# Transformer block on one core: epsilon inside the normalization statistics, waits sorted, and new instruction orders for four engines

## Chip, cores, metric

One core of one Trainium2 chip. The metric is the device time of one execution in microseconds (us). The kernel before takes 204.28 us, the median of 3 runs (204.25 to 204.39).

## The reference

The block takes x (1 x 2048 x 448, bf16) through linear attention with a feature map and then a gated MLP, each behind a normalization without weights:

```python
def _layernorm(x, axis=-1, eps=1e-5):
    return (x - mean(x)) / sqrt(var(x) + eps)

# attention, H = 16 heads of Dh = 28
q, k, v = split(x @ wqkv)
pq, pk = q @ w_phi, k @ w_phi                 # per head, 28 x 28
phi_q = concat(softmax(pq), softmax(-pq))
phi_k = concat(softmax(pk), softmax(-pk))
kv, z = phi_k^T v, sum_s phi_k
o = (phi_q kv) / (phi_q z + 1e-6)
A = o @ wo
# MLP, F = 1792
B = (sigmoid(x @ w_gate) * (x @ w_up)) @ w_down

h  = x + A(_layernorm(x))
h2 = h + B(_layernorm(h))
```

## The kernel before

The 2048 rows are 16 tiles of 128 rows; four tiles make a chunk of 512. Every step is an operation with a name, `op(engine, name, function, reads, writes)`. `Graph` derives the dependences from what is read and written. **The order on each engine is written out by hand** in `ORDER`, one string of names for each of SP (DMA issues), ACT, PE, DVE and POOL; each engine executes its string strictly in order. `Graph.emit` puts semaphore waits ahead of each operation: the list `o.waits` is walked in order, and each entry becomes one `wait_ge` on the engine's queue. In the kernel before, that list is sorted by the place of the producer in the program text, latest first. `schedule()` works out an order of all operations by passing over the engines again and again, without any times; `emit` uses it as `self.order`. Some operations allow several engines; the one whose string holds the name gets it.

The names that matter here, with t the tile:

- `x…` loads x. `bst t`, `agg t` (DVE, L514, L515) are `bn_stats` and `bn_aggr` of a tile; `ve1_a` adds EPS to the variance, `pow1_a` (POOL, L527) takes it to the power -0.5, `nm1_a` negates the mean, `nb1_a` multiplies the two for ACT. They run once for a group of tiles: 0, 1, 2, 3, 4 to 5, 6 to 7, 8 to 11, 12 to 15; a is the first tile. `xn t` (L540 on ACT, L543 elsewhere) writes the normalized tile to one of three slots of `xn_pad`; `xT t` transposes it, by PE and an evacuation `xT t e` for tiles 0 to 3, by a DMA on SP's queue after that (L553).
- `wT0..3` and their evacuations `wTe0..3` transpose the key weights; `w2m0_0..3` multiply them by `w_phi`, `w2e0_0..3` evacuate (L500). `w2m1`, `w2e1` do the same for the query weights. `warm0..9` are matmuls on zeros, with no use but to keep PE running.
- `ppa/ppb` and `vva/vvb` project keys and values for tiles 0 to 3 in pairs; `pva t`, `pvb t` do both for one tile from 4 on. The a and b halves write the same PSUM banks with other row halves of PE, so that b waits for a. `ek t` (ACT) takes both exponentials, `ss t`, `rs t` (DVE) their sums and reciprocals, `phi t` (POOL or DVE, L655) the product, `v1 t` copies v; `kva t`, `kvb t` (PE) add the tile to the key-value sums.
- `pqa/pqb c_i` project the queries of a chunk, `eq` (ACT) takes their exponentials. `kvzA..D` mask the sums into matmul operands; `qs` and `num t` are the queries' products with them; `rsm qq b c rden o` (DVE, `o` on POOL or DVE) normalize; `oT` transposes; `woa/wob` is the output projection, `h t` the residual. For tiles 0 and 1 the second normalization uses `bs2`, `ag2`, `ve`, `pow2`, `hn`, `hT`, as the first one; for the others `h` accumulates the sum, `nm` and `sq` follow.
- `ga c_f`, `gb c_f` are the gate and up projections of a group of tiles, `sig` and `hh` the gating, `dn/dp/dm` the down projection, `fin` and `out` the end.

Of the kernel before, what the change touches and what calls it, by code (L numbers as in the profile page):

```python
# [321 lines left out]
def build(nc, A_x, A_wqkv, A_w_phi, A_wo, B_w_gate, B_w_up, B_w_down, out):  # L322
# [10 lines left out]
    with ExitStack() as es:  # L333
# [183 lines left out]
        def rstd(ts):  # L517
# [3 lines left out]
            def fve(e):  # L521
                return e.tensor_scalar(ve1[:, a:b], mv1[:, a:b, 1], EPS, None, op0=ALU.add)  # L522
# [465 lines left out]
```

## Time and profile before

| what | us |
|---|---|
| median of 3 runs | 204.28 |
| profiled execution, first to last instruction | 202.8 |
| what lies around the span (204.28 less 202.8) | 1.5 |
| PE busy | 195.9 |
| DVE busy | 135.5 |
| ACT busy | 95.7 |
| POOL busy | 55.6 |
| first gate matmul `ga0_1` starts at | 60.59 |

The profile is of one execution whose own time is its span and the 1.5 around it; all times in the text count from the span's first instruction. Busy time is the union of an engine's instructions, so that PE counts as busy in the matmuls on zeros too. The granted PE clock is 1.000 throughout.

### The profile page before, as it was taken

The numbers are of one execution on the slowest core, as the hardware profiler recorded it, in microseconds if no ns is written. First come the engines' busy times: TensorE is split into PE (matmuls) and PEld (weight loads), VectorE is DVE, ScalarE is ACT, GpSimd is POOL, SyncE is SP. The second block draws the span as 40 slices with busy tenths as digits, with TensorE's granted clock in tenths as the row PEclk, the third lists the DMA queues.
The fourth block names the chain that finished last, engine by engine and source line by source line (L and its number), as shares of the span: only waits on it lengthen the run. The fifth ranks groups of instructions, "written<-read, shape, count | busy, mean of one in ns | idle before, by whom it ended". The sixth has DMA issues, their size and how long they took to land.

```text
span 202.8 us, 5881 instructions
## 1 busy us (share of the span) xinstructions
PE 195.9 (97%) x2508; PEld 109.4 (54%) x2508; DVE 135.5 (67%) x328; ACT 95.7 (47%) x191; POOL 55.6 (27%) x97
## 2 busy tenths in 40 slices
PE   7889999999979999999999999999999999999995
PEld 3734556665448776677444444444554555454443
DVE  5899999979998897858667967536432422272224
ACT  3887989988882527222333342324422212222220
POOL 5599699723144303700033020001400000000000
DMA  6985516849949411251004411030212000004003
GB/s 154 316 141 123 80 33 89 230 158 279 308 37 229 55 31 29 50 82 26 3 3 100 100 29 26 3 74 24 58 47 54 0 0 3 0 3 136 0 0 94
DMA packets 32867, 16.27 MB, mean 80 GB/s; under 512 B 25096, under 2 KB 31944, under 8 KB 32840
## 3 DMA queue, kind: packets, MB, share of 16 engines
q1 hardware_dynamic: 32336, 15.86, 34.9%
q8 instruction: 20, 0.33, 0.7%
q10 hardware_dynamic: 504, 0.03, 0.2%
q14 instruction: 7, 0.06, 0.1%
HBM read 8.34 MB, written 1.84 MB: 50 GB/s over the span
## 4 chain that ended last, share of the span: by engine, by line
PE 84%; DVE 8%; POOL 2%; DMA 2%; issue 1%; SPq 1%; ACT 0%; DVEq 0%
PE psum L305 78%; PE psum L909 5%; DVE st L514 2%; DMA x_sb<-in_A_x_dram 2%; DVE ss L645 2%; POOL o_pad L780 1%; DVE b_sb L771 1%; DVE xn_pad L543 1%; SPq L407 1%; DVE c_sb L774 1%; PE psum L507 0%; POOL xn_pad L543 0%; DVE rs L651 0%; DVE xnT L500 0%; POOL rst L527 0%
## 5 line engine op out<-in xcount | busy, mean ns | idle before, releaser
L305 PE MATMUL psum<-xnT,wg_sb 64*128 64x512 bf16 (+1 forms) x490 | 93.1, 334 | 0.3 <-DVE rden L776 0.2
L305 PE MATMUL psum<-xnT,wu_sb 64*128 64x512 bf16 (+1 forms) x490 | 92.9, 334 | 0.0
L881 ACT ACTIVATE sg_sb<-psum 128x512 bf16<-128x512 f32 (+1 forms) x70 | 34.8, 511 | 91.4 <-PE psum L305 90.9
L882 DVE SCALAR_TENSOR_TENSOR hhT<-sg_sb,psum 128x512 bf16<-128x512 bf16 (+1 forms) x70 | 38.9, 576 | 53.3 <-ACT sg_sb L881 53.0
L305 PEld LDWEIGHTS psum<-xnT,wg_sb 64*128 64x128 bf16 x490 | 44.4, 94 | 23.4 <-DVE hhT L882 4.8
L305 PEld LDWEIGHTS psum<-xnT,wu_sb 64*128 64x128 bf16 x490 | 44.4, 94 | 13.5
L305 PE MATMUL psum<-wd_sb,hhT 64*128 64x448 bf16 x336 | 36.8, 350 | 0.0
L305 PEld LDWEIGHTS psum<-wd_sb,hhT 64*128 64x128 bf16 x336 | 16.9, 94 | 15.1 <-DVE x_sb L806 0.5
L305 PE MATMUL psum<-Wk,xnT 64*128 64x448 bf16 x112 | 22.1, 351 | 0.3 <-ACT Wk L500 0.2
L305 PE MATMUL psum<-wv_sb,xnT 64*128 64x448 bf16 x112 | 22.2, 351 | 0.1
L815 POOL TENSOR_SCALAR ve<-ssq 128x1 f32<-128x1 f32 x11 | 2.6, 233 | 57.8 <-ACT junk L812 57.5
L655 POOL TENSOR_TENSOR phi<-hhT,rs 128x896 bf16<-128x896 bf16 x10 | 17.3, 1749 | 3.6 <-DVE ve L522 1.8
L645 DVE TENSOR_REDUCE ss<-hhT 128x32 f32<-128x896 bf16 x16 | 16.9, 1063 | 0.3 <-ACT hhT L642 0.3
L691 ACT ACTIVATE eq<-psum 120x1024 bf16<-120x1024 f32 x16 | 15.7, 1028 | 1.3 <-PE psum L305 1.1
L305 PE MATMUL psum<-xnT,Wq 64*120 64x512 bf16 x112 | 15.0, 385 | 0.1
L305 PE MATMUL psum<-wo_o,oT 64*128 64x448 bf16 x56 | 13.2, 350 | 0.0
L305 PE MATMUL psum<-wo_e,oT 64*128 64x448 bf16 x56 | 13.2, 349 | 0.0
L916 DVE SCALAR_TENSOR_TENSOR x_sb<-psum,x_sb 128x448 bf16<-128x448 f32 (+2 forms) x17 | 9.4, 591 | 2.7 <-PE psum L909 1.6
L909 PE MATMUL psum<-wd_sb,hhT 128*128 128x448 bf16 (+2 forms) x70 | 11.2, 316 | 0.0
L305 PEld LDWEIGHTS psum<-Wk,xnT 64*128 64x128 bf16 x112 | 7.8, 94 | 6.1 <-PE psum L305 0.5
L780 POOL TENSOR_TENSOR o_pad<-c_sb,rden 128x448 bf16<-128x448 bf16 x8 | 7.4, 935 | 11.1 <-DVE rden L776 11.0
L771 DVE TENSOR_TENSOR b_sb<-psum,qq 128x464 bf16<-128x464 f32 x16 | 10.2, 638 | 0.3
(99 smaller groups left out, 236.9 us busy)
## 6 DMA issues: line engine op xcount, KB each, us to landing
out_dram<-x_sb SPq DMA_DIRECT2D x15, 112.0 KB, 1.8
x_sb<-in_A_x_dram SPq DMA_DIRECT2D x7, 224.0 KB, 4.6
wd_sb<-in_B_w_down_dram SPq DMA_DIRECT2D x7, 224.0 KB, 4.4
wg_sb<-in_B_w_gate_dram SPq DMA_DIRECT2D x3, 448.0 KB, 5.5
wu_sb<-in_B_w_up_dram SPq DMA_DIRECT2D x3, 448.0 KB, 5.9
wv_sb<-in_A_wqkv_dram SPq DMA_DIRECT2D x2, 224.0 KB, 4.9
wk_sb<-in_A_wqkv_dram SPq DMA_DIRECT2D x2, 196.0 KB, 3.8
wo_e<-in_A_wo_dram SPq DMA_DIRECT2D x1, 336.0 KB, 3.2
```

The source lines that it names most:

```text
L305: p = e.matmul(o, lhsT=w, rhs=r, start=st, stop=sp, tile_position=(row, 0))
L514: op("dve", "bst%d" % t, lambda e: e.bn_stats(st1[:, t, :], x_sb[:, t, :]), r=[("x", t)], w=[("st1", t)])
L645: op("dve", "ss%d" % t, lambda e: e.tensor_reduce(ss[:, s, :].rearrange("p (b h) -> p b h", h=2), eks.rearrange("p b (d h) -> p b h d", h= ...
L655: return e.tensor_tensor(phi[:, sp, :, :, :].rearrange("p b a n -> p (b a) n")[:, :, 0:56].rearrange("p b (d h) -> p b d h", h=2), eks.rea ...
L691: op("act", "eq%d_%d%s" % (c, i, "pm"[sg]), lambda e, sg=sg: e.activation(eq[c][:, sg, 2 * i:2 * i + 2, :].rearrange("p g n -> p (g n)"), ...
L771: op("dve", "b%d" % t, lambda e: e.tensor_tensor(h3(b_sb), OMv[:, :, :, 0:EV], h2(qq)[:, :, :, None].to_broadcast([P, NB, 8, EV]), ALU.mul ...
L780: return e.tensor_tensor(o_pad[:, t % NO, off:off + D].rearrange("p (h d) -> p h d", h=H), c_sb[:, t % NS, :, 0:DH], rden[:, t % NS, :][:, ...
L815: op(("pool", "dve"), "ve%d" % t, lambda e: e.tensor_scalar(ve2[:, t:t + 1], ssq2[:, t:t + 1], 1.0 / D ** 3, EPS, op0=ALU.mult, op1=ALU.ad ...
L881: op("act", "sig" + nm, lambda e: e.activation(sg_sb[:, k, 0:N], bk(bg)[:, 0:N], ACT.Tanh, scale=0.5), r=[B(bg)], w=[("sg", k)])
L882: op("dve", "hh" + nm, lambda e: e.scalar_tensor_tensor(out=hhT[(t0 // 4) % NHH][:, ff, ns], in0=sg_sb[:, k, 0:N], scalar=1.0, in1=bk(bu)[ ...
L909: p = e.matmul(bk(b)[:, lo:hi], lhsT=hb[:, ff, TS(t)], rhs=wd_sb[:, ff, lo:hi], start=ff == 0, stop=ff == FT - 1)
L916: op("dve", "fin%d%s" % (t, nm), lambda e: e.scalar_tensor_tensor(out=h_sb[:, t, lo:hi], in0=bk(b)[:, lo:hi], scalar=0.5, in1=h_sb[:, t, l ...
```

## The change

`bn_stats` leaves six numbers for a tile, and `bn_aggr` combines them. The buffers get nine columns: the last three, written once by `steps`, are a third group with count 0, mean 0 and a sum of squares of D x EPS, so that the aggregated variance already contains EPS. `ve1` and, for tiles 0 and 1, `ve` are gone; `xn` subtracts the mean instead of adding a negated one, so `nm1` is gone; `nb1` is made per tile and only where `xn` runs on ACT, which is nowhere in the new orders. The waits of an operation are sorted: loads first, then by the place of the producer in `self.order`. ACT, PE, DVE and POOL get new orders up to the second gate group; behind what is shown here they are the same names in the same order. SP's order is the same.

```diff
     @staticmethod
+    def engine(name):
+        return next(e for e in ENGINES if name in ORDER[e].split())
...
         known = {e: {} for e in ENGINES}
+        rank = {i: n for n, i in enumerate(self.order)}
...
             o.waits = [j for j in o.waits if ops[j].dma is not None or ops[j].pos == last[ops[j].eng]]
+            o.waits.sort(key=lambda j: (ops[j].dma != "in", rank[j]))
...
-    "act": (
-        "wphi3 wphi2 wphi1 wphi0 par kvzones wTe0 wTe1 xT1e xT0e wTe2 w2e0_0 w2e0_1 w2e0_2 w2e0_3 xn3 xn4 ek0 ek1 "
-        "xn6 v1_1 v1_0 ek2 v1_2 v1_3 ek3 w2e1_1 w2e1_0 ek4 v1_4 w2e1_2 ek5 v1_5 ek6 v1_6 xn11 ek7 w2e1_3 xn12 ek8 "
-        "ek9 v1_9 ek10 v1_10 xn15 ek11 v1_11 ek12 v1_12 eq0_0m ek13 eq0_0p ek14 v1_14 ek15 v1_15 eq0_1p eq0_1m "
-        "eq1_0m kvzB eq1_0p eq1_1p eq1_1m eq2_0p oT0e oT1e eq2_1p eq2_0m eq2_1m h0 h1 eq3_0p eq3_0m eq3_1m eq3_1p "
-        "sig0_1 sig0_0 sig0_3 sig0_2 sig0_5 sig0_4 sq3 sq2 "
-        ...
+    "act": (
+        "wphi3 wphi2 wphi1 wphi0 kvzones wTe1 xT1e xT0e wTe3 w2e0_1 w2e0_3 xT3e ek0 ek1 v1_0 v1_1 ek3 ek2 v1_2 "
+        "v1_3 w2e1_1 w2e1_0 v1_4 ek4 ek5 v1_5 w2e1_2 w2e1_3 ek6 v1_6 ek7 v1_7 ek8 v1_8 ek9 v1_9 ek10 v1_10 ek11 "
+        "eq0_0p ek12 v1_12 ek13 v1_13 eq0_0m ek14 ek15 v1_15 eq0_1p eq0_1m eq1_0m kvzC kvzA eq1_0p eq1_1m eq1_1p "
+        "eq2_0p eq2_0m oT1e eq2_1p eq2_1m h1 h0 eq3_0m eq3_0p eq3_1p eq3_1m sig0_1 sig0_0 sig0_3 sig0_2 sig0_5 "
+        "sig0_4 sq2 sq3 "
+        ...
-    "pe": (
-        "warm0 warm1 warm2 wT0 wT1 xT1 warm3 xT0 warm4 warm5 wT2 w2m0_0 wT3 warm6 w2m0_1 w2m0_2 warm7 w2m0_3 "
-        "warm8 ppa0 warm9 ppb0 xT3 xT2 vva0 vvb0 ppa2 ppb2 vva2 vvb2 w2m1_0 w2m1_1 seed pva4 kva0 pvb4 pva5 "
-        "w2m1_2 w2m1_3 pvb5 pva6 kvb0 kva1 pvb6 kvb1 kva2 pva7 kvb2 kva3 pvb7 pva8 kvb3 kva4 pvb8 pva9 pqa0_0 "
-        "pvb9 pva10 kvb4 kva5 pvb10 kvb5 kva6 pva11 kvb6 kva7 pvb11 pva12 kvb7 kva8 pvb12 pqb0_0 pva13 kvb8 kva9 "
-        "pvb13 pva14 kvb9 kva10 pvb14 pva15 kvb10 kva11 pvb15 kvb11 kva12 pqa0_1 kvb12 pqb0_1 kva13 pqa1_0 kvb13 "
-        "kva14 pqb1_0 kvb14 kva15 kvb15 qs pqa1_1 num0 pqb1_1 num1 pqa2_0 num2 pqb2_0 pqa2_1 oT0 oT1 pqb2_1 num3 "
-        "woa0 wob0 num4 pqa3_0 pqb3_0 pqa3_1 num5 pqb3_1 hT0 hT1 num6 ga0_1 ga0_0 gb0_1 gb0_0 woa2 num7 ga0_3 "
-        "ga0_2 gb0_3 gb0_2 wob2 ga0_5 ga0_4 gb0_5 gb0_4 woa4 ga0_7 ga0_6 gb0_7 gb0_6 num8 wob4 "
-        ...
+    "pe": (
+        "warm0 warm1 wT1 wT0 warm2 xT1 warm3 warm4 warm5 warm6 warm7 xT0 wT2 wT3 w2m0_0 w2m0_1 w2m0_2 w2m0_3 "
+        "warm8 warm9 xT3 ppa0 ppb0 xT2 vva0 vvb0 ppa2 ppb2 vva2 w2m1_1 vvb2 seed w2m1_0 pva4 kva0 pvb4 pva5 kvb0 "
+        "kva1 pvb5 kvb1 pva6 w2m1_2 w2m1_3 pvb6 pva7 pqa0_0 pvb7 kva2 pva8 kvb2 kva3 pvb8 kvb3 pva9 kva4 pvb9 "
+        "kvb4 pva10 pqb0_0 pvb10 kva5 pva11 kvb5 kva6 pvb11 kvb6 pva12 kva7 pvb12 kvb7 pva13 kva8 pvb13 kvb8 kva9 "
+        "pva14 kvb9 kva10 pvb14 pva15 kvb10 kva11 pvb15 pqa0_1 kvb11 kva12 pqb0_1 pqa1_0 kvb12 kva13 pqb1_0 kvb13 "
+        "kva14 kvb14 kva15 kvb15 qs pqa1_1 num0 pqb1_1 num1 pqa2_0 num2 pqb2_0 pqa2_1 oT0 oT1 num3 pqb2_1 woa0 "
+        "wob0 num4 pqa3_0 pqb3_0 pqa3_1 num5 pqb3_1 hT1 hT0 num6 ga0_1 ga0_0 gb0_1 gb0_0 woa2 num7 ga0_3 ga0_2 "
+        "gb0_3 gb0_2 wob2 ga0_5 ga0_4 gb0_5 gb0_4 woa4 ga0_7 ga0_6 gb0_7 gb0_6 wob4 num8 "
+        ...
-    "dve": (
-        "zero bd0 mask2 bst1 agg1 ve1_1 bst0 agg0 nm1_0 xn1 xn0 bst2 agg2 bst3 agg3 bst4 bst5 wTe3 agg4 agg5 bst6 "
-        "bst7 agg6 agg7 bst10 ve1_6 agg10 nm1_6 bst8 bst11 bst9 agg8 xT3e agg11 agg9 xT2e nm1_8 ve1_8 ss0 ss1 rs0 "
-        "bst13 rs1 ss2 bst12 bst14 rs2 agg12 agg13 agg14 bst15 ss3 xn10 ss4 rs3 agg15 rs4 ve1_12 nm1_12 phi3 ss5 "
-        "rs5 v1_7 ss6 phi5 rs6 v1_8 ss7 ss8 rs7 rs8 phi7 ss9 rs9 ss10 rs10 ss11 rs11 ss12 rs12 v1_13 ss13 phi12 "
-        "rs13 ss14 rs14 ss15 phi14 rs15 phi15 kvzA kvzC kvzD rsm0 qq0 b0 c0 b1 rden0 c1 rsm2 rden1 qq2 b2 c2 "
-        "rden2 o2 rsm3 qq3 b3 c3 rden3 bs2_0 rsm4 ag2_0 qq4 bs2_1 b4 ag2_1 c4 hn0 rsm5 qq5 hn1 b5 hT1e c5 hT0e "
-        "rden4 rden5 rsm6 qq6 b6 c6 hh0_1 hh0_0 rsm7 rden6 qq7 b7 hh0_3 hh0_2 h2 h3 c7 hh0_5 hh0_4 nm2 rden7 o7 "
-        "nm3 hh0_7 hh0_6 h5 h4 hn3 rsm8 hh0_9 qq8 hh0_8 hn2 b8 c8 hh0_11 hh0_10 h7 h6 rsm9 "
-        ...
+    "dve": (
+        "zero bd0 steps bst1 agg1 mask2 bst0 agg0 xn1 wTe0 bst3 bst2 agg3 wTe2 bst4 w2e0_0 agg2 w2e0_2 bst5 agg4 "
+        "bst10 agg5 bst6 bst7 xT2e agg6 bst9 agg7 ss0 bst8 rs0 agg9 ss1 bst11 bst13 rs1 agg10 bst12 agg8 agg11 "
+        "ss2 ss3 xn8 rs3 rs2 bst14 ss4 ss5 phi3 bst15 agg14 agg12 rs4 agg15 agg13 phi4 ss6 rs6 rs5 ss7 rs7 ss8 "
+        "phi6 ss9 rs8 rs9 ss10 v1_11 rs10 phi8 phi9 ss11 rs11 ss12 rs12 ss13 v1_14 rs13 ss14 par ss15 rs14 rs15 "
+        "phi14 phi15 kvzD rsm0 kvzB qq0 b0 c0 b1 rden0 c1 rsm2 rden1 qq2 b2 c2 oT0e rden2 rsm3 qq3 b3 c3 rden3 "
+        "bs2_0 rsm4 bs2_1 qq4 ag2_1 ag2_0 b4 c4 hn1 hn0 rsm5 qq5 b5 hT1e c5 hT0e rden4 rden5 rsm6 qq6 b6 c6 hh0_1 "
+        "hh0_0 rsm7 rden6 qq7 b7 hh0_3 hh0_2 h3 h2 c7 hh0_5 hh0_4 rden7 o7 ve2 hh0_7 hh0_6 h5 h4 rsm8 nm3 nm2 "
+        "hh0_9 qq8 hh0_8 b8 c8 hh0_11 hh0_10 h6 rsm9 h7 "
+        ...
-    "pool": (
-        "neghalf ident0 ident phipad wqpad epsl0 epsr0 nm1_1 pow1_1 ve1_0 pow1_0 nm1_2 ve1_2 ve1_3 v1ones pow1_3 "
-        "nm1_3 pow1_2 nb1_3 ve1_4 nm1_4 pow1_4 nb1_4 opad0 nb1_2 xn2 pow1_6 xn5 nb1_6 pow1_8 nb1_8 xn7 phi0 phi1 "
-        "xn8 xn9 phi2 phi4 pow1_12 nb1_12 xn13 phi6 xn14 phi8 phi9 phi10 phi11 phi13 o0 o1 ve0 pow2_0 o3 ve1 "
-        "pow2_1 o4 o5 o6 ve3 pow2_3 ve2 pow2_2 "
-        ...
+    "pool": (
+        "opad0 neghalf v1ones ident0 ident pow1_1 phipad pow1_0 xn0 wqpad pow1_3 xn3 pow1_2 xn2 epsl0 epsr0 "
+        "pow1_4 xn5 xn4 pow1_6 xn6 phi0 xn7 phi1 pow1_8 xn9 phi2 xn10 xn11 pow1_12 xn13 xn12 phi5 xn14 phi7 xn15 "
+        "phi10 phi11 phi12 phi13 o0 o1 o2 o3 pow2_1 pow2_0 o4 o5 o6 pow2_2 ve3 hn2 pow2_3 hn3 "
+        ...
...
-        st2 = sb("st2", [P, 2, 6], f32)
+        st2 = sb("st2", [P, 2, 9], f32)
...
-        st1 = sb("st1", [P, NT, 6], f32)
+        st1 = sb("st1", [P, NT, 9], f32)
...
+        def steps(e):
+            for st in (st1, st2):
+                e.memset(st[:, :, 6:8], 0.0)
+                p = e.memset(st[:, :, 8:9], D * EPS)
+            return p
+        op(("dve", "pool"), "steps", steps, w=["steps"])
...
-            op("dve", "agg%d" % t, lambda e: e.bn_aggr(mv1[:, t, :], st1[:, t, :]), r=[("st1", t)], w=[("mv1", t)])
+            op("dve", "agg%d" % t, lambda e: e.bn_aggr(mv1[:, t, :], st1[:, t, :]), r=[("st1", t), "steps"], w=[("mv1", t)])
...
-            op("pool", "pow1_%d" % a, lambda e: e.tensor_tensor(rst1[:, a:b], ve1[:, a:b], neghalf[:, 0:n], ALU.pow),
-               r=[("ve1", a), "neghalf"], w=[("rst1", a)])
...
+            op("pool", "pow1_%d" % a, lambda e: e.tensor_tensor(rst1[:, a:b], mv1[:, a:b, 1], neghalf[:, 0:n], ALU.pow),
+               r=[("mv1", t) for t in ts] + ["neghalf"], w=[("rst1", a)])
...
-                return e.tensor_scalar(dst, src, nm1[:, t:t + 1], rst1[:, t:t + 1], op0=ALU.add, op1=ALU.mult)
+                return e.tensor_scalar(dst, src, mv1[:, t, 0:1], rst1[:, t:t + 1], op0=ALU.subtract, op1=ALU.mult)
...
-                op(("dve", "pool"), "ve%d" % t, lambda e: e.tensor_scalar(ve2[:, t:t + 1], mv2[:, t % 2, 1:2], 1.0, EPS, op0=ALU.mult,
-                                                                          op1=ALU.add), r=[("mv2", t)], w=[("ve2", t)])
+                op("pool", "pow2_%d" % t, lambda e: e.tensor_tensor(rst2[:, t:t + 1], mv2[:, t % 2, 1:2], neghalf[:, 0:1], ALU.pow),
+                   r=[("mv2", t), "neghalf"], w=[("rst2", t)])
```

## The prediction

> **What bounds the kernel now.** I read the page's busy shares first, then the chain that ended last, then the busy time by stage, then the timelines of the engines ahead of the points where PE waits. Names such as `pva4` are the program's operations; each is found in a timeline by its place in the engine's order.
>
> The page, and the tail of the chain that ended last (start, length, what):
>
> ```profile
> PE 195.9 (97%) x2508; PEld 109.4 (54%) x2508; DVE 135.5 (67%) x328; ACT 95.7 (47%) x191; POOL 55.6 (27%) x97
> ```
>
> ```profile
> 25.45 19.21 PE psum L305 x360
> ...
> 60.59 4.79 PE psum L305 x86
> 65.38 0.04 issue
> 65.42 60.41 PE psum L305 x858
> ```
>
> From 60.59, where the first gate matmul `ga0_1` starts, PE runs without a hole, and its order from there differs by one swap (`wob4`, `num8`). PE's work is the same 2508 matmuls. So the change can only move the moment at which `ga0_1` starts; the 142.2 us behind it stay.
>
> Busy time by stage; the cuts are the starts of `pva4` (18.66, first steady projection), `qs` (44.83, end of the key-value sums) and `ga0_1`:
>
> ```profile
> 0.00:18.66 18.66, 16.09 (x158) 8.59 (x159) 15.32 (x45) 12.99 (x25) 13.62 (x41) 1.00 0.86 193
> 18.66:44.83 26.17, 25.79 (x476) 15.19 (x476) 25.05 (x46) 24.55 (x52) 19.71 (x15) 1.00 0.51 114
> 44.83:60.59 15.76, 14.17 (x256) 7.82 (x253) 14.60 (x41) 14.04 (x18) 4.34 (x8) 1.00 0.85 208
> ```
>
> The columns after the length are PE, PEld, DVE, ACT, POOL. Stage 1 hides its slack under warm-up matmuls, which count as busy; stage 2 is PE's own pace with DVE and ACT 94% to 96% busy beside it; stage 3 is a ping-pong of PE with DVE and ACT, PE 90%.
>
> **Stage 1, to `pva4`.** ACT, DVE, PE and POOL, in that order, at the decisive places:
>
> ```profile
> 7.65 0.53 ACT L500 COPY WkT<-psum 112x448 bf16<-112x448 bf16 x1 [0.45 <-PE psum L569]
> 8.08 2.32 ACT L500 CAST Wk<-psum 128x448 bf16<-128x448 f32 x4
> 10.26 0.81 ACT L540 ACTIVATE xn_pad<-x_sb,nb,rst 128x512 bf16<-128x512 bf16 x1
> 8.91 0.37 DVE L500 COPY WkT<-psum 112x448 bf16<-112x448 bf16 x1
> 10.46 0.93 PE L305 MATMUL psum<-Wk,xnT 64*128 64x448 bf16 x8 [0.25 <-ACT Wk L500]
> 12.01 0.77 POOL L543 TENSOR_SCALAR xn_pad<-x_sb,nm,rst 128x512 bf16<-128x512 bf16 x1
> ```
>
> Nothing can start before the key weights land (7.16), the same in both. Then:
> - `wTe3` leaves DVE, where it sat behind statistics until 8.91, for ACT, free at 7.84: WkT is whole at 8.37, not 9.28. `w2m0_3` then runs at about 8.5 (9.34).
> - The four `w2e0` took 2.32 in a row on ACT. Two go to DVE, priced at the row of the same shape without the reordering (v copy, 0.56): 8.47 to 9.58. ACT's two, 0.67 each, end at 9.7. `ppa0` goes at 9.76 instead of 10.46: -0.70.
> - `warm9` no longer stands between `ppa0` and `ppb0` (1.08 apart; neighbours such as `vva0`/`vvb0` are 1.00 apart), and ACT has lost `xn3` and `xn4` (0.81 each), which delayed `ek0`. `ppb0` ends at 11.5, `ek0` and `ek1` (0.98, overlapped 0.1) at 13.4, so `ppa2` starts at 13.46 (14.74): -1.28.
> - From there ACT sets the pace: `ppb2` ends at 15.2, `ek3` and `ek2` take to 17.1, `v1_2` (0.53) to 17.55. Here `ek2` is a new thing in front of `v1_2`. `pva4` waits for it: **17.6, -1.05**.
>
> The cover: all `xn` but two now run on POOL (0.77, about what ACT took). POOL loses the EPS and negation steps (`ve1`, `nm1`, 0.15 to 0.24 each) and the `nb1` products; the `pow1` (0.57 one column, 0.71 two, 1.00 four) stay. Its chain `pow1_3 xn3 pow1_2 xn2`, two small fills, `pow1_4 xn5 xn4` ends at about 13.4; `xT4` takes 3.15 to land (12.34 to 15.49 before): 16.6, a margin of 1.0. That is 1.1 later than before, and what stands behind it on SP's queue waits with it: eleven transposes and the load of the last x tiles; `xT5` to `xT8` then land 1.4 to 2.3 ahead of their `pva`. If that cover went, each microsecond at `xT4` would cost one. The four fills called `steps` lie where DVE idles 1.03 waiting for x. No row shows an aggregate over nine columns; six cost 0.18, so I bound it by 0 and by half as much again, 0.09 each, 18 of them spread over 50 us: 0 on the path, at most 0.2.
>
> **Stage 2, `pva4` to `qs`.** PE's own pace. Going away: the hole before `kva3` (0.32 idle, 0.47 counting the pitch) and three short waits of 0.1. Coming in: `pva` to `pvb` takes 1.00 at least (18.66 to 19.66), so a lone `kv` group beside it wastes 0.12 (three more such tiles: 0.36), and `kva14`, `kvb14` are now adjacent (0.34 against 0.11, as `kva15`, `kvb15` are): 0.23; one waste of 0.11 goes. Net -0.2 to +0.1; I take **-0.1**. This holds if the producers keep pace. ACT is relieved by six `xn` (4.3). DVE gives `xn10` (1.75) for `xn8`, three v copies for two and four small statistics steps for nothing, and takes one `phi` more (0.61): walked along its new order, `phi15` ends 0.2 before PE wants it. The new wait here is `xn8` for `pow1_8`, which POOL reaches at 20.1: DVE stands for 0.4 with `rs3`, `rs2`, `bst14` and `ss4` queued behind; `rs2` ends at 21.6 and frees `phi2`, done at 23.3, which `kva2` wants at 24.9. So it costs nothing while 1.6 are spare. POOL gets eight `xn` (6.0) for one `xn` (0.75), fourteen small steps (2.7) and one `phi` (1.65): +0.9. Its tightest point is `phi5` behind `xn13` and `xn12`: done at 30.1 to 30.4, wanted by `kva5` at 30.5; further on it has 0.3 to 0.5.
>
> **Stage 3, `qs` to `ga0_1`.** `o2` (0.62 on DVE, ahead of `rsm3`) goes to POOL, in exchange for `oT0e` (0.42): `c3` releases `num4` earlier. `ve0`, `ve1` (0.19 each and a hand-over of 0.08) vanish between the aggregate and `pow2`, so `hn1`, `hn0` fit before `rsm5`, and `hn1` (0.41) no longer lies inside `rsm5` to `c5`, which releases `num6` (PE idle 1.06 before it). That is -0.25. The rows on DVE just ahead of `ga0_1`:
>
> ```profile
> 59.26 0.63 DVE L774 TENSOR_TENSOR c_sb<-b_sb,psum 128x464 bf16<-128x464 bf16 x1
> 59.80 0.42 DVE L500 COPY xnT<-psum 128x512 bf16<-128x512 bf16 x1
> 60.14 0.36 DVE L776 RECIPROCAL rden<-c_sb 128x16 f32<-128x16 bf16 x2
> ```
>
> The copy is `hT0e`. `ga0_1` starts 0.37 after `hT0e` ends (60.22), where a single wait is answered in 0.08 (`xn1` 5.13, `xT1` 5.21): after `hT0e` it still steps through eight waits for loads that landed by 55.02. With the loads first, -0.3. Elsewhere in the kernel PE does not stand at such a list. Together **-0.55**. Behind it, `hn2` and `hn3` move to POOL (0.77 against 0.41 on DVE) and `nm2` behind `rsm8`; in the old clock `hT2` would go out at 72.7 (73.08) and `hT3`, held by the 1.95 that SP took to issue `hT2`, at 74.6 (75.03). `hT3` had landed 0.24 before `ga2_1` wanted it, so this tight place gets looser: nothing.
>
> **Sum.** -1.05 - 0.1 - 0.55 = -1.7. The profiled execution has 202.8 from first to last instruction; the runs' median is 204.28, so 1.45 lies around the span and stays. 202.8 - 1.7 + 1.5 = **202.6**. A difference of 0.2% (0.4 us) is about what a measurement of this kernel tells from no change.
>
> **Rivals.**
> - *POOL a little late.* Transposes landed in 2.4 to 4.1 us (`xT9`: 22.02 to 26.11). If `xT10` takes 4.1, `xn13` slips by 1.3, `phi5` with it, and PE stands for up to 1.1 at `kva5`: 203.7. For: margin 0.1. Against: eight of the twelve transposes took 3.15 or less. Chance 0.16.
> - *Saturated DVE keeps the gain.* If the DVE share of `w2e0` takes 0.67 as on ACT and `xn8` meets a long POOL step as `xn10` did, DVE is 0.2 + 1.3 later, of which 0.2 is margin: 1.3 lost, 203.9, no change. Chance 0.09.
> - *POOL and DVE slow each other: slower.* These rows, DVE then POOL, are one step that elsewhere takes 0.41 and one that elsewhere takes 1.69:
>
> ```profile
> 21.50 1.75 DVE L543 TENSOR_SCALAR xn_pad<-x_sb,nm,rst 128x512 bf16<-128x512 bf16 x1
> 24.86 2.08 POOL L655 TENSOR_TENSOR phi<-hhT,rs 128x896 bf16<-128x896 bf16 x1 [1.76 <-DVE ve L522]
> ```
>
>  Both lay beside a long step of the other engine. The new order puts 9 `phi` and about 10 `xn` on POOL between 13.4 and 41 with DVE full beside it. At 0.39 each, as in the second row, POOL would slip by 7.4; it decides from a mean of 0.13, where 2.4 of slip eats the 0.3 of margin and the 1.7 and adds 0.4. At 0.2: 206. For: those rows. Against: DVE's `ss` and `bst` steps, most of its work, ran beside POOL's `phi0` and `phi1`, which took 1.69 both. I counted 0.3 to 0.4 for each `phi` of DVE that meets POOL, no more. Chance 0.14.
>
> The Trainium skill speaks for that last rival: its page "GPSIMD Engine Reference", section Key points, says that GpSimd shares its SBUF interfaces with VectorE and that the two contend where a DVE instruction runs in a two-port mode or reads two SBUF inputs. The trace agrees in the two rows above. By that rule the seven DVE `phi` and `xn8` would cost POOL and DVE time and `ss` and `bst`, one SBUF input each, would not; so by rule and by rows alike the sum stays at 202.6, and 206 takes a wider effect than the page states.
>
> That the sort does not put the latest last (it follows an order worked out without times) costs at most the 0.3 and stays in the forecast, whose own chance is 0.61.
>
> **Range.** The forecast's own is 201.8 (stage 3 and the holes give 0.8 more) to 203.3. To leave out no more than 2 in 10 it takes in the first rival and the better part of the second: 201.8 to 204.2. Faster by over 0.2%: forecast and first rival, 0.77; within: 0.09; slower: 0.14.
>
> **What would show it.** Right: `ppa0` near 9.8, `ppa2` near 13.5, `pva4` near 17.6, `qs` near 43.5, `ga0_1` near 58.9, and under 0.1 between the end of `hT0e` and `ga0_1`. Wrong: PE waiting for POOL `phi` (L655 by its new number) between 25 and 42, POOL `phi` means above 1.9, or PE holes behind 61.

## The result, and the profile after

The changed kernel takes 219.26 us (median of 4 runs, 218.79 to 221.3) beside 204.26 for the kernel before: a ratio of 1.077, interval 1.072 to 1.082 (a ratio weighs every run; that of the two medians is 1.073). It is 7.7% slower; the forecast was 202.6 with a range to 204.2. Its profiled execution has a span of 217.4 and a time of 219.28, so 1.9 lies around it. In one kernel below, three of twelve executions were in a slower state, more than 1.5% above its fastest, and its median and ratio leave them out.

The page's busy shares and slices after; PE still makes its 2508 matmuls, but POOL is busy for 76.1 (55.6 before), and the granted clock, at full speed throughout before, dips to 6 tenths in two slices:

```profile
PE 200.4 (92%) x2508; PEld 113.7 (52%) x2508; DVE 135.2 (62%) x324; ACT 90.8 (42%) x184; POOL 76.1 (35%) x89
...
PE   7986697197999799999999999999999999999995
...
POOL 5999999999324422345000502000140000000000
PEclk9999699969999999999999999999999999999999
```

Busy time by stage after, cut at `pva4` (21.34), `qs` (59.49) and `ga0_1` (74.97); the columns are PE, PEld, DVE, ACT, POOL, then the granted clock:

```profile
0.00:21.34 21.34, 16.77 (x158) 9.26 (x159) 15.93 (x45) 12.02 (x25) 18.12 (x28) 1.00 0.59 145
21.34:59.49 38.15, 29.58 (x474) 16.87 (x476) 25.44 (x44) 21.51 (x43) 34.17 (x20) 0.91 0.37 91
59.49:74.97 15.48, 14.07 (x256) 8.00 (x253) 13.84 (x40) 13.26 (x19) 4.87 (x7) 1.00 1.01 264
```

Stage 1 is 2.7 longer, stage 2 12.0, stage 3 0.3 shorter, and the part behind `ga0_1` 0.2 longer (142.4, from 142.2): together 14.6, the difference of the spans. Stage 2 was PE's own pace and is now POOL's: POOL is busy for 34.17 of 38.15. Of its 12.0, 8.2 are idle time of PE (38.15 less 29.58 is 8.6; before it was 0.4), and 3.8 are the same matmuls taking longer (29.58 against 25.79). In two stretches of 3.41 the granted clock was 0.50 (the rows stand in the last section). PE was busy for 6.24 of these 6.82; as an estimate, half of that, 3.1 of the 3.8, comes of the clock, and the rest is open.

What PE waited for, summed by releaser (total, times, longest), and the stretch of POOL that leads into stage 2:

```profile
PE psum L309 <- POOL phi L657: 6.1, 3, 4.4
PE psum L309 <- DMA xnT<-xn_pad: 4.3, 3, 2.0
...
PE psum L517 <- POOL xn_pad L543: 1.1, 2, 0.6
```

```profile
14.62 4.13 POOL L543 TENSOR_SCALAR xn_pad<-x_sb,mv,rst 128x512 bf16<-128x512 bf16 x2
18.72 0.72 POOL L531 TENSOR_TENSOR rst<-mv,neghalf 128x2 f32<-128x2 f32 x1
19.55 2.08 POOL L543 TENSOR_SCALAR xn_pad<-x_sb,mv,rst 128x512 bf16<-128x512 bf16 x1
21.59 1.69 POOL L657 TENSOR_TENSOR phi<-hhT,rs 128x896 bf16<-128x896 bf16 x1
23.26 2.07 POOL L543 TENSOR_SCALAR xn_pad<-x_sb,mv,rst 128x512 bf16<-128x512 bf16 x1
```

POOL has no gap above 0.11, and each `xn` takes 2.07 where the prediction paid 0.77. `phi` is at its old 1.69. The groups of the page say the same over the whole run:

```profile
L543 POOL TENSOR_SCALAR xn_pad<-x_sb,mv,rst 128x512 bf16<-128x512 bf16 x14 | 29.5, 2111 | 0.9 <-POOL rst L531 0.4
...
L657 POOL TENSOR_TENSOR phi<-hhT,rs 128x896 bf16<-128x896 bf16 x9 | 15.1, 1686 | 0.2 <-PE psum L309 0.2
```

Fourteen `xn` at 2.11 instead of 0.77 to 0.81 are some 18 us more of POOL. Three things had changed in that step at once: it subtracts where it added, it reads the mean from `mv1` in place instead of from `nm1`, and it runs beside a fuller DVE.

### The profile page after: what moved, and what is told of

The parts are those of the page before. It is cut to its first block, busy times and chain, and to the rows that moved or that the text cites. A ratio compares the mean times of both kernels' runs of the same rounds, so it can differ in the third digit from the quotient of the medians.

```text
span 217.4 us, 5863 instructions
## 1 busy us (share of the span) xinstructions
PE 200.4 (92%) x2508; PEld 113.7 (52%) x2508; DVE 135.2 (62%) x324; ACT 90.8 (42%) x184; POOL 76.1 (35%) x89
## 4 chain that ended last, share of the span: by engine, by line
PE 72%; POOL 18%; ACT 4%; DMA 2%; issue 2%; DVE 2%; POOLq 0%
PE psum L309 64%; POOL xn_pad L543 12%; PE psum L911 5%; POOL phi L657 4%; ACT eq L693 3%; POOL rst L531 2%; PE psum L503 2%; DMA xnT<-xn_pad 2%; ACT kvz L726 1%; DVE st L801 1%; DVE st L524 0%; PE psum L571 0%; ACT x_sb L802 0%; PE psum L517 0%; DVE WkT L510 0%
## 5 line engine op out<-in xcount | busy, mean ns | idle before, releaser
L543 POOL TENSOR_SCALAR xn_pad<-x_sb,mv,rst 128x512 bf16<-128x512 bf16 x14 | 29.5, 2111 | 0.9 <-POOL rst L531 0.4
L309 PE MATMUL psum<-Wk,xnT 64*128 64x448 bf16 x112 | 25.3, 379 | 4.5 <-DMA xnT<-xn_pad 4.3
L309 PE MATMUL psum<-wv_sb,xnT 64*128 64x448 bf16 x112 | 25.5, 379 | 0.1
L309 PEld LDWEIGHTS psum<-wd_sb,hhT 64*128 64x128 bf16 x336 | 17.6, 94 | 14.5 <-DVE x_sb L808 0.5
L817 POOL TENSOR_SCALAR ve<-ssq 128x1 f32<-128x1 f32 x10 | 2.0, 202 | 54.4 <-ACT junk L814 54.0
L657 POOL TENSOR_TENSOR phi<-hhT,rs 128x896 bf16<-128x896 bf16 x9 | 15.1, 1686 | 0.2 <-PE psum L309 0.2
L643 ACT ACTIVATE hhT<-psum 128x448 bf16<-128x448 f32 x16 | 8.8, 552 | 13.8 <-PE psum L309 7.4
L309 PE MATMUL psum<-v,phi 64*128 64x58 bf16 x256 | 8.0, 193 | 6.3 <-POOL phi L657 6.1
L782 POOL TENSOR_TENSOR o_pad<-c_sb,rden 128x448 bf16<-128x448 bf16 x9 | 8.3, 936 | 14.4 <-DVE rden L778 14.3
L309 PEld LDWEIGHTS psum<-v,phi 64*128 64x128 bf16 x256 | 7.2, 99 | 11.7 <-POOL phi L657 6.0
```

Of the source, the lines that this page charges most:

```text
L309: p = e.matmul(o, lhsT=w, rhs=r, start=st, stop=sp, tile_position=(row, 0))
L543: return e.tensor_scalar(dst, src, mv1[:, t, 0:1], rst1[:, t:t + 1], op0=ALU.subtract, op1=ALU.mult)
L643: e.activation(ek[:, s, :, 0, :], src, ACT.Exp)
L657: return e.tensor_tensor(phi[:, sp, :, :, :].rearrange("p b a n -> p (b a) n")[:, :, 0:56].rearrange("p b (d h) -> p b d h", h=2), eks.rea ...
L782: return e.tensor_tensor(o_pad[:, t % NO, off:off + D].rearrange("p (h d) -> p h d", h=H), c_sb[:, t % NS, :, 0:DH], rden[:, t % NS, :][:, ...
```

## The experiments

Times are medians; ratios are to the kernel before, run on the same chip, and weigh every run, so that a few long runs can bring a ratio above 1 where the medians are equal. Profiles are of one execution each. The labels e1 to e14 are those of the expectations.

**Is it the subtraction, the operand, or DVE beside it?** Four kernels. The first (e1) only replaces the operation of POOL's `xn` in the changed kernel:

```diff
-  e.tensor_scalar(dst, src, mv1[:, t, 0:1], rst1[:, t:t + 1], op0=ALU.subtract, op1=ALU.mult)
+  e.tensor_scalar(dst, src, mv1[:, t, 0:1], rst1[:, t:t + 1], op0=ALU.add, op1=ALU.mult)
```

> The changed kernel; on POOL alone, xn adds the mean where it subtracted it (same operands, so its values are wrong; DVE's two xn still subtract). Theory 1, the subtraction itself is slow on POOL: xn there falls from 2.08 us to 0.77 and the kernel to 201.8 to 204.2 (the prediction's range, 202.6 likeliest). Theory 2, the mean read in place out of the aggregate (every second column) is slow: xn stays at 2.08 and the kernel at 219. Theory 3, POOL is slowed by DVE's work beside it: 2.08 and 219 as well.

Measured: 204.56, ratio 1.003 (1.001 to 1.006), `xn` back at 0.77 (eleven of fourteen; the longest took 1.14). One word of the step is worth 14.7 us. The second (e2) gives POOL a negated mean to add:

```diff
+  nm1_a on DVE, seven times: tensor_scalar(nm1[:, a:b], mv1[:, a:b, 0], -1.0, None, op0=ALU.mult)
+  xn on POOL: tensor_scalar(dst, src, nm1[:, t:t + 1], rst1[:, t:t + 1], op0=ALU.add, op1=ALU.mult)
```

> The changed kernel, with the negated mean brought back for POOL's xn alone: seven small DVE steps (0.1 each), POOL adds it; DVE's two xn subtract in place. Theory 1 and theory 2 both expect xn on POOL at 0.77 and 202.0 to 204.2; theory 3 expects 2.08 and 219. If the new orders are worth what was predicted, it is faster than before by 1 to 2.4 us; if they are worth nothing, 204.3.

Measured: 208.23, ratio 1.019 (1.016 to 1.022). `xn` took 0.77 again, but `pva4` to `qs` took 29.2: the seven steps stand in DVE's full order, one of them, of four columns, took 1.14 beside a `phi` of POOL, and DVE's `phi9` took 2.10 instead of 0.61 beside another (how, the kernel with the negation on POOL shows below). The third (e3) is the kernel before with its POOL `xn` subtracting (it has seven there, not the eight that the expectation counts):

```diff
-  e.tensor_scalar(dst, src, nm1[:, t:t + 1], rst1[:, t:t + 1], op0=ALU.add, op1=ALU.mult)
+  e.tensor_scalar(dst, src, mv1[:, t, 0:1], rst1[:, t:t + 1], op0=ALU.subtract, op1=ALU.mult)
```

> The kernel before, old orders, with its eight xn on POOL subtracting the mean in place. Theory 1 and 2: each takes 2.08 for 0.77, 1.3 more; POOL was busy 19.7 of 26.2 us in the stage from pva4 to qs, so that some 3 to 8 us appear in the whole: 207 to 212. Theory 3 (it comes of the new orders): 0.77 and 204.3.

Measured: 211.52, ratio 1.037 (1.034 to 1.040), 2.18 a step. In the old orders the same step costs 7.3 us. The fourth (e4) puts ten steps behind one another on POOL, in the kernel before, behind its last use:

```diff
+  tensor_scalar(mo, mi, a, b, op0, op1) with add or subtract, in first or second place,
+  the scalar from nm1, from mv1 or a constant, over 512 and 256 columns
```

> The kernel before with ten tensor_scalar steps on POOL behind its last one, one at a time, on 512 or 256 bf16 columns. Theory 1: every form with a subtraction takes 2.1 (1.1 at 256 columns), every other 0.77 (0.4), wherever its scalars lie. Theory 2: those two that read the mean in place take 2.1, the others 0.77. Theory 3: all 0.77. The kernel's time says nothing, since the steps lie behind the rest on POOL.

Measured; the groups of that kernel on these lines (`add` from `nm1`, `subtract` from `nm1`, `subtract` from `mv1`, `add` from `mv1`, `mult` then `add`, `mult` then `subtract`; `subtract` and `add` with constants; `subtract` and `add` over 256 columns):

```profile
L954 POOL TENSOR_SCALAR mo<-mi,nm,rst 128x512 bf16<-128x512 bf16 x1 | 0.8, 767 | 0.1
L956 POOL TENSOR_SCALAR mo<-mi,nm,rst 128x512 bf16<-128x512 bf16 x1 | 2.1, 2093 | 0.1
L958 POOL TENSOR_SCALAR mo<-mi,mv,rst 128x512 bf16<-128x512 bf16 x1 | 2.2, 2206 | 0.1
L960 POOL TENSOR_SCALAR mo<-mi,mv,rst 128x512 bf16<-128x512 bf16 x1 | 0.8, 767 | 0.1
L962 POOL TENSOR_SCALAR mo<-mi,rst,nm 128x512 bf16<-128x512 bf16 x1 | 0.8, 767 | 0.1
L964 POOL TENSOR_SCALAR mo<-mi,rst,nm 128x512 bf16<-128x512 bf16 x1 | 2.1, 2082 | 0.1
L966 POOL TENSOR_SCALAR mo<-mi 128x512 bf16<-128x512 bf16 x1 | 1.9, 1932 | 0.1
L968 POOL TENSOR_SCALAR mo<-mi 128x512 bf16<-128x512 bf16 x1 | 0.6, 617 | 0.1
L970 POOL TENSOR_SCALAR mo<-mi,nm,rst 128x256 bf16<-128x256 bf16 x1 | 1.2, 1222 | 0.1
L972 POOL TENSOR_SCALAR mo<-mi,nm,rst 128x256 bf16<-128x256 bf16 x1 | 0.6, 553 | 0.1
```

Wherever a `subtract` stands in the step, it is slow; where its scalar lies makes a difference of 0.11 to 0.16 at most, and nothing else changed. DVE isn't needed for it: it stood idle throughout the `subtract` with constants (155.76 to 157.69). From 256 to 512 columns the sum grows by 0.84 ns a column, the difference by 3.40. So the subtraction itself is shown to be the cause; why POOL needs longer for it no run shows.

**What is left at 204.56?** The rest of the change was to bring 1.7 us and brought none. Four more kernels, three of them on the first with `add`. The first (e5) puts `par` back on ACT:

```diff
-  ORDER["dve"]: ... ss14 par ss15 rs14 rs15 phi14 phi15
+  ORDER["dve"]: ... ss14 ss15 rs14 rs15 phi14 phi15;   ORDER["act"]: ... kvzones par wTe1
```

> The changed kernel with `add` in POOL's `xn` (values wrong, as in the earlier run of that form: 204.56) and with `par`, the copy of 128x2 that makes the mask for the query sums, back on ACT behind `kvzones`. Theory port hold: on DVE this copy of a few elements took 1.14 because it began while POOL's `phi13` ran and stood until that ended; what stood behind it (`ss15`, `phi14`, `phi15`) made PE wait 0.58 and 0.16 before `kva14` and `kva15`. With it on ACT those two stalls go, `pva4` to `qs` falls from 26.8 to about 26.2 and the time by 0.6 to 0.7: 203.9. Rival, DVE is just full there and `par` counts with its 0.1: 204.4 to 204.6 and the stalls before `kva14` stay.

Measured: 204.83, ratio 1.003 (1.000 to 1.005). The runs spread over 2.6 us and do not show it, but the profile does: `pva4` to `qs` is 26.09, from 26.82, and both stalls are gone. These are the lines of DVE (first) and POOL in the kernel with `par` on DVE:

```profile
40.04 1.09 DVE L650 TENSOR_REDUCE ss<-hhT 128x32 f32<-128x896 bf16 x1
41.04 1.14 DVE L449 CAST par<-mask 128x2 bf16<-128x2 f32 x1
42.09 1.07 DVE L650 TENSOR_REDUCE ss<-hhT 128x32 f32<-128x896 bf16 x1
```

```profile
37.17 4.98 POOL L660 TENSOR_TENSOR phi<-hhT,rs 128x896 bf16<-128x896 bf16 x3
```

A copy of two columns, over at 42.18, 0.03 after POOL's `phi13` (37.17 + 4.98 = 42.15). On ACT it took 0.19. The Trainium skill, page "SBUF — State Buffer", section "SBUF: two separate sides", says that VectorE and GpSimd share a port pair, that it goes to whichever begins first for its whole instruction, and that the other is blocked until then; of VectorE's steps this concerns those in a two-port mode or with two SBUF inputs. The trace agrees: `ss`, with its one input, ran beside three `phi` at 1.03 to 1.09 and did not stand, and `par` stood until the end.

The next (e6) moves the eight weight waits to `hT0`, and the one after it (e8) leaves out the sort:

```diff
+  for b in range(4): for a in "gu": g.ops[at["hT0"]].deps[at["ld_w%s%d" % (a, b)]] = False
```

> As e5, and the eight waits for the gate and up weights stand at `hT0`, two PE operations ahead of `ga0_1`, where PE has 0.95 of idle time behind them. Theory count: what `ga0_1` pays behind `num6` is the number of waits that PE's sequencer steps through there (ten, some 0.03 each), whatever their order; with two left, the gap from the end of `hT0e` to `ga0_1` falls from 0.32 to under 0.1 and the time by 0.25 to 0.3 against e5: 203.6. Rival, the gap is the last wait's own latency or the weight load of the new matmul group: gap 0.3 and time as in e5, 203.9.

```diff
-  o.waits.sort(key=lambda j: (ops[j].dma != "in", rank[j]))
```

> The changed kernel with `add` in POOL's `xn` (values wrong), without the line that sorts the waits. By the prediction's step the sort is worth 0.3 at `ga0_1`: the gap from the end of `hT0e` rises from 0.32 to 0.6 and the time from 204.56 to 204.9. By the theory that the number of waits counts and not their order: gap 0.3, 204.5, no change.

Measured: 204.30, ratio 1.002 (0.999 to 1.005), and 204.85, ratio 1.003 (1.000 to 1.006). The runs of both spread over some 3 us, so the medians decide nothing here; the profiles do. PE at `num6` and `ga0_1`, with `par` on ACT (first) and with the waits moved as well:

```profile
59.28 0.40 PE L324 MATMUL psum<-kvz,eq 56*128 56x60 bf16 x16 [0.95 <-DVE c_sb L794]
59.88 0.27 PE L324 MATMUL psum<-xnT,wg_sb 64*128 64x256 bf16 x1 [0.19 <-ACT eq L711]
```

```profile
59.25 0.40 PE L324 MATMUL psum<-kvz,eq 56*128 56x60 bf16 x16 [0.94 <-DVE c_sb L794]
59.67 0.27 PE L324 MATMUL psum<-xnT,wg_sb 64*128 64x256 bf16 x1
```

From start to start 0.60 falls to 0.42. Without the sort it is 0.59, with it 0.60 (changed kernel: 74.37 to 74.97). So the number of waits behind `num6` counts, and their order is worth nothing. In the old orders the same move, further down, gives 0.42 from 0.64. The reading that fits: PE gets to the list only once `num6` is gone, which `c5` releases late, and then it has to step through all ten.

The last of the four (e7) puts the negation on POOL:

```diff
+  ORDER["pool"]: pow1_a nm1_a, seven times;   par on ACT;   weight waits at hT0
```

> The changed kernel with right values: seven small steps `nm1` on POOL behind `pow1` make the negated means again, POOL's `xn` adds them, `par` on ACT and the weight waits at `hT0` as in e6. If POOL takes the seven steps (0.15 each, 1.1 in all, less the 0.1 that it idles between `pow1` and `xn`) into its idle 1.1 before `xn11` and 0.9 before `phi10`: as e6, 203.6, faster than before by 0.3%. If POOL is the bound by then, up to 1.1 of it reaches PE at `kva13`: 204.7. On DVE the same seven steps gave 208.2.

Measured: 205.4, ratio 1.005 (1.004 to 1.007). The time is on the rival's side, but not for its reason. PE idled 0.76 before `kva9`, for `phi9`, which is DVE's, and 0.49 before `kva11`, for `phi11`. `phi9` on DVE and `phi10` on POOL here, then the same two in e6:

```profile
35.32 2.10 DVE L683 TENSOR_TENSOR phi<-hhT,rs 128x896 bf16<-128x896 bf16 x1
35.20 1.74 POOL L683 TENSOR_TENSOR phi<-hhT,rs 128x896 bf16<-128x896 bf16 x1 [0.43 <-PE psum L327]
```

```profile
34.83 0.61 DVE L675 TENSOR_TENSOR phi<-hhT,rs 128x896 bf16<-128x896 bf16 x1
35.15 1.83 POOL L675 TENSOR_TENSOR phi<-hhT,rs 128x896 bf16<-128x896 bf16 x1 [1.13 <-PE psum L324]
```

Begun 0.12 behind POOL's step, DVE's took 2.10; begun 0.32 ahead, 0.61. `rs11` stands behind it on DVE, and POOL then idled 2.01 for `rs11` before `phi11`: POOL was not full. The seven steps took 0.22 to 0.24 each. In e2 the same two steps met in the same way (`phi9` 0.20 behind, 2.10).

**The change with the slow step repaired, and one part of it alone.** The negation on ACT (e9):

```diff
+  op("act", "nm1_%d" % a, lambda e: e.activation(nm1[:, a:b], mv1[:, a:b, 0], ACT.Identity, scale=-1.0), ...)
+  par on ACT;   weight waits at hT0
```

> The changed kernel with right values: POOL's `xn` adds the negated mean again, and the seven steps `nm1` that make it run on ACT (about 0.2 each, put where ACT idles 0.15 to 0.9), `par` on ACT, weight waits at `hT0`. Theory: with the subtraction off POOL, and no step added to POOL or DVE, the new orders run as in e6 (span 202.1, `pva4` to `qs` 26.1 and `qs` to `ga0_1` 15.3): 203.6 to 204.4, no change or 0.2% faster than before. Rival: the hand-over from a third engine holds POOL's `xn`, as the seven steps on DVE (208.2) and on POOL (205.4) did: 205 or more, with PE waits before `kva5` to `kva11`.

Measured: 204.32, ratio 1.000 (0.998 to 1.001): the repaired change is worth nothing. Stage 3 is 15.30, 0.46 shorter than before; stage 2 is 26.34 (0.17 of it a wait of `pva12` for ACT's copy `v1_10`); POOL's `xn` waited for none of the negations; and behind `ga0_1` there is a new wait of 0.2, `ga2_1` for `hT3`. For that one (e10):

```diff
-  ORDER["pool"]: pow2_2 ve3 hn2 pow2_3 hn3
+  ORDER["pool"]: ve3 pow2_3 ve2 pow2_2;   ORDER["dve"]: ... nm2 rden7 o7 nm3 ... h4 hn3 ... hh0_8 hn2
```

> As e9, with `hn2` and `hn3` back on DVE in the old places. In the new order the transposes `hT2` and `hT3` start 1.4 apart and took 4.5 to 4.7 and 3.6 to 4.0 to land, against 3.0 and 2.5 when they started 1.95 apart, and `ga2_1` waited up to 0.3 for them. Theory, overlap: started apart, `hT3` lands 16.9 after `ga0_1` starts, as before, not 17.1 to 17.4, and `ga2_1` waits less than 0.1: 0.1 to 0.3 less than e9. Rival, transposes take what they take: `hT2` starts 0.47 later and `hT3` lands 0.3 to 0.5 later, `ga2_1` waits 0.4 or more: 0.2 to 0.4 more than e9.

Measured: 204.40, ratio 1.000 (0.998 to 1.001). In the profile the wait is gone: `hT2` and `hT3` start 1.65 apart instead of 1.39, take 2.7 and 2.9 instead of 3.4 and 3.9, and `hT3` lands 17.0 after `ga0_1` starts, not 17.3. Issued later, it lands earlier. Stage 2 took 26.59 this time (0.42 of it a wait of `pva12` for `xT12`, which took 4.61 to land), and the median shows nothing of the gain.

Then the epsilon alone, in the old orders (e11), and the same with the weight waits at `hT1` (e12):

```diff
-  ve1_a (eight), ve0, ve1;   st1, st2 with six columns
+  steps;   st1, st2 with nine columns;   pow1, pow2 from mv1, mv2
```

> The kernel before with one part of the change alone: epsilon goes into the statistics (aggregates over nine columns), the eight `ve1` and `ve0`, `ve1` go, the old orders stay. By the prediction's pricing this part shortens the small chain aggregate, `pow`, normalised x, by 0.15 to 0.27 a time and costs nothing by itself: stage 1 0.1 to 0.3 shorter and stage 3 up to 0.1, time 203.9 to 204.2. Rival: nothing on the path hangs on these steps: 204.3, and if aggregates of nine columns take longer (0.09 each, sixteen on a full DVE), stage 2 is up to 0.5 longer: 204.8.

> As e11, and the eight weight waits at `hT1`, the PE operation ahead of `num6`. If the count of waits behind `num6` is what `ga0_1` pays, as e6 against e5 shows (0.32 down to 0.14), the gap from `hT0e` to `ga0_1` falls from 0.37 to about 0.15 here too: 0.2 less than e11, 203.8. Rival: in the old order `hT1` is evicted ahead of `c5`, so waits stepped through there delay `c5` and `num6` by as much: no gain.

Measured: **203.47**, ratio 0.995 (0.993 to 0.997), and **203.43**, ratio 0.997 (0.995 to 0.998). Both beat both kernels. Stage 2 of the first, by the same columns as above:

```profile
17.89:43.45 25.56, 25.50 (x476) 15.14 (x476) 24.02 (x45) 24.23 (x52) 20.11 (x16) 1.00 0.54 125
```

It is 0.6 shorter than before, and the 0.3 that PE waited for DVE's `phi3` are gone. Stage 1 is shorter too, 17.89 from 18.66, but that is not shown to come of the epsilon: the last key weights landed at 6.37 instead of 7.16 in this execution, and `wT2` began at 6.56 instead of 7.21. In the second kernel, whose stage 1 is the same, `wT2` began at 7.51 and stage 1 took 18.48. DVE (first) and POOL at the place of the 0.6:

```profile
20.14 1.07 DVE L662 TENSOR_REDUCE ss<-hhT 128x32 f32<-128x896 bf16 x1
21.13 0.41 DVE L560 TENSOR_SCALAR xn_pad<-x_sb,nm,rst 128x512 bf16<-128x512 bf16 x1
21.44 1.08 DVE L662 TENSOR_REDUCE ss<-hhT 128x32 f32<-128x896 bf16 x1
```

```profile
21.32 1.75 POOL L672 TENSOR_TENSOR phi<-hhT,rs 128x896 bf16<-128x896 bf16 x1
```

`xn10` began 0.19 ahead of `phi2`, took 0.41 and cost POOL 0.06, less than the 0.22 for which the two overlapped: this way round the hold is not a full one. Before, `phi2` came first:

```profile
21.41 1.69 POOL L655 TENSOR_TENSOR phi<-hhT,rs 128x896 bf16<-128x896 bf16 x1
```

`xn10` began at 21.50, 0.09 behind (its row stands in the prediction), stood until `phi2` ended at 23.10 and took 1.75. In the second of the two kernels `xn10` began 0.26 behind and took 1.58, and its profiled execution took 204.1. So it is a race of two engines. In the two profiles in which DVE wins it (e11, e14) stage 2 took 25.56; in the three of the old orders in which it loses (before, e4, e12) 26.07 to 26.49. That the removed steps make DVE win more often, and that the spread of the runs comes from the race, is argued, not shown; nor do its 0.6 make up the whole 1.0 between the medians.

**Where stage 1 and stage 3 went.** Two more (e13, then e14):

```diff
-  ORDER["pe"]: ... warm4 warm5 warm6 warm7 xT0 wT2 wT3 w2m0_0 .. w2m0_3 warm8
+  ORDER["pe"]: ... warm4 xT0 wT2 wT3 w2m0_0 .. w2m0_3 warm5 warm6 warm7 warm8
```

> As e9, with the warm-up matmuls `warm5`, `warm6` and `warm7` moved from ahead of `xT0` and `wT2` to behind `w2m0_3`. The prediction had `wT2` start when the key weights land (7.16); in e9 they landed at 6.88 and `wT2` started at 7.82, behind eight warm-ups and two transposes that PE ran at half its later pace. Theory, PE's own list: without the 1.06 of the three warm-ups ahead of it, `wT2` starts 0.6 to 0.9 earlier, `ppa0` and `pva4` follow (`pva4` 17.5 to 17.7 instead of 18.30) and the time falls by 0.6 to 0.8: 203.6. Rival, the reordering of the weights (`w2e0` on DVE and ACT) or `xn3`, `xn2` on POOL set `ppa0` and `ppa2`: `pva4` stays within 0.2 of 18.3, time 204.3.

```diff
+  the kernel with epsilon alone; behind eq1_0m (ACT), phi15 (DVE), qs (PE) and phi13 (POOL) the new orders
```

> As e11, and from `qs` on the new orders of ACT, DVE, PE and POOL (`o2` on POOL, `oT0e` and `hn1`, `hn0` on DVE ahead of `rsm5`), with `hn2`, `hn3` on DVE and the weight waits at `hT0` as in e10. Theory: the new orders lose in stage 2 (26.3 in e9 against 25.6 in e11) and win in stage 3 (15.3 against 15.8), so joined at `qs` they give stage 3 15.3 and, less the 0.15 that the part behind `ga0_1` lost in e10, 0.3 less than e11: 203.2. Rival: stage 3's gain comes from what stage 2 left free (DVE and ACT less behind) or is given back at `ga2_1`: 203.5, as e11.

The first measured 204.91, ratio 1.002 (1.000 to 1.005), with `pva4` at 18.96: it fits neither theory. `wT2` did start 0.6 earlier (7.22, 0.05 after its weights landed), but the warm-ups, now behind `w2m0_3`, and a PE that came to full pace only at about 7.2 held `ppa0` until 11.07. It doesn't settle the matter. What its profile shows by chance is the prediction's first rival; POOL:

```profile
24.19 0.77 POOL L571 TENSOR_SCALAR xn_pad<-x_sb,nm,rst 128x512 bf16<-128x512 bf16 x1
26.65 1.09 POOL L571 TENSOR_SCALAR xn_pad<-x_sb,nm,rst 128x512 bf16<-128x512 bf16 x1 [1.68 <-DMA xnT<-xn_pad]
27.70 1.00 POOL L553 TENSOR_TENSOR rst<-mv,neghalf 128x4 f32<-128x4 f32 x1
29.55 1.52 POOL L571 TENSOR_SCALAR xn_pad<-x_sb,nm,rst 128x512 bf16<-128x512 bf16 x2 [0.84 <-DMA xnT<-xn_pad]
31.03 2.05 POOL L686 TENSOR_TENSOR phi<-hhT,rs 128x896 bf16<-128x896 bf16 x1
```

`xT8` and `xT9` started 1.23 apart and took 4.57 and 4.00; POOL's `xn11` and `xn13` stood for 1.68 and 0.84, `phi5` ended at 33.08, and `kva5` waited 1.0 for it. The prediction had that rival at `xT10`; here the two before it were late.

The second measured 203.61, ratio 0.995 (0.993 to 0.998): no more than epsilon alone. Behind `num0` the new orders save 0.64 (13.63 from 14.27), 0.23 of it by the weight waits; but `num0` itself comes 0.54 later behind `qs` (2.03 from 1.49), because its operand `kvzA` is now on ACT, which is still at work there (on `eq` until 44.34, while `qs` starts at 43.70). The rival is right: the new stage 3 needs what the new stage 2 leaves free on ACT.

## Why the prediction was wrong

The step that failed is the **cover of stage 1 and stage 2: "all `xn` but two now run on POOL (0.77, about what ACT took)"**. The row of 0.77 was of a step that adds a negated mean; the change makes it subtract, and no row of before showed a `subtract` on POOL. Nor was it bounded: DVE's `hn1`, a subtraction at 0.41, and POOL's rows of other forms would have been the nearest. The text counted POOL's margin at 0.3, against fourteen such steps: 0.02 more for each eats it. They took 1.3 more. That made POOL the bound of stage 2, which the prediction had as PE's own pace, and is 14.7 of the 16.7 us between forecast and result.

Of the marks that were to show it right, none held: `ppa0` came at 11.06, `ppa2` at 15.35, and from the end of `hT0e` to `ga0_1` it is still 0.32. Of those that were to show it wrong, one came: PE waited 6.1 for POOL's `phi`, while the mean of `phi` stayed at 1.69.

Its rivals: that POOL and DVE slow each other had the right side and the right place (PE waiting for POOL's `phi`), but not the mechanism; `phi` took 1.69, not over 1.9, and POOL's `subtract` was as slow (1.93) while DVE idled. What it did have is an effect at single places that the text priced too low: "0.3 to 0.4 for each `phi` of DVE that meets POOL, no more" was 1.5 for `phi9` in e2 and e7. That POOL is a little late by its transposes came true in e13 alone. The saturated DVE did not come: `xn8` met no long step and took 0.41.

Without the subtraction, the other terms of the sum (from one profile of the kernel with `par` on ACT, span 202.5):

- **Stage 1, -1.05: measured -0.35.** The steps were priced rightly. From `wT2` to `ppa0`, from there to `ppa2` and from there to `pva4` the prediction has 2.6, 3.7 and 4.1; with the negation on ACT they took 2.59, 3.68 and 4.21. The start of `wT2` was wrong: 7.16, when its weights land, "the same in both". In the new order `wT2` stands behind eight warm-ups, and starts at 7.82 or at 6.96 by the pace at which PE runs these. Nor is the landing the same: over the sixteen profiles it lies between 6.15 and 7.35, whatever the kernel. In the nine profiles with PE's new order ahead of it (e13 left out) `wT2` begins at 7.6 in the mean, in the six with the old one at 7.0. So the new steps are some 0.9 shorter and begin some 0.6 later, and a single stage 1 can be off by half a microsecond by luck. The same eight transposes of key weights, and `wT2`, `wT3` behind them, in the kernel without the sort (first) and with the negation on ACT:

```profile
4.82 0.58 PE L573 MATMUL psum<-ident,wk_sb 112*112 112x112 bf16 x8
...
6.96 0.58 PE L573 MATMUL psum<-ident,wk_sb 112*112 112x112 bf16 x8
```

```profile
5.09 0.95 PE L597 MATMUL psum<-ident,wk_sb 112*112 112x112 bf16 x8
...
7.82 0.58 PE L597 MATMUL psum<-ident,wk_sb 112*112 112x112 bf16 x8
```

 The first kernel reached `pva4` at 17.40, 0.2 ahead of the forecast; the second at 18.30. The granted clock reads 1.00 in both, so only the pace shows it: in the first, matmuls over 512 columns go from one every 0.427 us to one every 0.216 at about 4.5; in the second, those over 128 columns from 0.107 to 0.056 at about 6.3. The Trainium skill, page "TensorE: Matmul & The Clock Gate", section "What's actually happening", says that the clock rises at the end of a window that doesn't start with the kernel, so that the moment varies by half a microsecond either way; the two profiles, 1.8 apart, differ by more than that.
- **Stage 2, -0.1: measured -0.08** with `par` on ACT. The `par` on DVE, +0.73, was nowhere in the prediction: it does not name that move, though the rule of the shared interfaces was on the table, and applied to `phi` and `xn8` alone. The margin of 0.1 at `phi5` was rightly seen as tight (e13 broke it); that `phi9` begins only 0.3 ahead of `phi10` (e6), the place that cost time in e2 and e7, was not seen.
- **Stage 3, -0.55: measured -0.28.** The new order of DVE's steps was to give 0.25 and gave 0.23 (from `qs` to `num6`, 15.11 to 14.88). The 0.3 for the sorted waits came to nothing, 0.32 with the sort and without. Taken off that place they gave 0.18.
- **Behind `ga0_1`, 0: measured +0.4** (140.63 from `ga0_1` to the last step of DVE, 140.22 before). "This tight place gets looser" was wrong: `hT2` starts earlier, but closer to `hT3`, both took longer, and `hT3` landed later; `ga2_1` started 17.47 after `ga0_1` instead of 17.16, 0.3 of the 0.4.

Together -0.3, as the spans say (202.5 from 202.8), where the sum had -1.7. The part that did pay by itself, epsilon in the statistics, has no term of its own in the sum; the hole before `kva3`, which the prediction counted as going away, is gone in it without the new orders.

## What to carry to other kernels

A price taken from a row holds for the operation of that row: when a step moves to another engine or changes its operation word, look for a row with that word on that engine, and where there is none, bound it and multiply by the count before anything else. Before filling an engine that shares a port, walk its neighbour's small copies too: what they cost is set by the length of the step they meet and by which of the two begins first, not by their own. And a list of waits costs by its length wherever the operation ahead of it is released last; move waits that are long met to an operation with idle time behind it.
